# A state-exchange and feed-forward kernel: the first batch in a new order, one maximum for both halves, ScalarE's low words without a bias operand

## The chip, the cores and the metric

The kernel runs on one core of one Trainium2 chip. The metric is the device time of one execution in microseconds; lower is better. TensorE (PE) multiplies matrices, and its weight loads (PEld) run beside the products. VectorE (DVE) and ScalarE (ACT) do the elementwise work, GpSimd (POOL) almost nothing here, and SyncE (SP) issues nearly all transfers. A queue written SPq is SyncE's own sequence of transfers.

## The reference

The inputs are x (8 batches, 8 heads, 512 tokens, 64 features), state (8, 8, 32 rows, 64), moe_w_in (512 x 2048) and moe_w_out (2048 x 512), all float32. For each batch and head there are two attentions:

```
scores  = x state^T / 8;   a  = softmax(scores);   xread = a state      (512 tokens read 32 states)
scores2 = state x^T / 8;   a2 = softmax(scores2);  sread = a2 x         (32 states read 512 tokens)
```

The two results are joined to 544 rows a batch, with the heads side by side as 512 features, and go through a feed-forward layer: h = rows @ w_in; g = h where h >= 1, 0 where h <= -1, (h + 1)^2 / 4 between; out = g @ w_out. The output has 4352 rows of 512.

## The kernel before

**Tiling.** One batch's 512 tokens are the columns of its products. The hidden layer of 2048 is cut into 8 chunks j of 256. The product a @ (state @ w_in) is used in place of (a @ state) @ w_in: for each chunk, state @ w_in is made first (step sw, line 380). Values that must be exact are split into a high and a low part, and three products are added (lines 445 to 447 for the hidden layer, step p; lines 521 to 523 for the output, step g2). The state rows of all batches go through the layer as a ninth batch at the end.

**Steps of one chunk.** p.0.b.j and p.1.b.j are the two halves of the hidden product; relu (ACT, line 462), square (ACT, 466) and bound (DVE, 469) make u; gh (ACT, 478 and 620) and gl (DVE, 483) split it; g2.0 and g2.1 are the two halves of the output product. The two PSUM buffers of p come free when bound has read them. The weights come packed: the raw chunk i.c of w_in or o.c of w_out is loaded, its high words are scaled on ScalarE (high, line 575), its low words turned into small integers on ScalarE (line 567) or VectorE (562), and both are joined by VectorE (line 587: step w.c for w_in, join.c for w_out). woh.c and wol.c split the joined w_out. Raw chunks of w_in share two buffers, and a buffer comes free with step w of the chunk in it.

**Attention of one batch.** sc are the scores of both attentions at once (line 217). The first softmax goes turn (224), top1, less1, exp1, sum1, inv1, norm1, back (264), and ath and atl split its result. The second goes top2 (281 and 282: a maximum along the row, then a multiplication), exp2 (285), then a transpose of its result. In batch 0 TensorE transposes (e2p, kept.0). In every later batch VectorE transposes blocks of 32 x 32 (turn_blocks, line 310; steps blocks.1.0 and blocks.1.1 for batch 1), and then SyncE moves the blocks to their places with 16 transfers of 32 KB (shuffle, lines 312 to 324; step dma.eb.1). read2 (line 334) multiplies the result with the tokens xn, which SyncE loads (line 189; steps dma.xn.0 and dma.xn.1).

**Order.** All of batch 0, with the start of batch 1, is issued in an order written out by hand: SEQ holds one list of steps for each of SyncE, TensorE, VectorE and ScalarE, and each engine does its list strictly in that order. A planner (Plan.times, line 50) plays the lists with costs written beside each step and interleaves them; where TensorE would be idle between sc.0.1 and the first g2, it puts in filler matmuls (line 165), one for each 0.34 us planned. A step of the plan waits only for the steps named in its `after` list and for buffers. Nothing in the plan comes after dma.eb.1 or dma.xn.1. Their user is issued behind the plan, in the main loop: at chunk 0 of batch 1 the loop issues the hidden products of that chunk, then the places called "mid", and only then the output product of the chunk before (chunk 7 of batch 0). The line that puts read2 of batch 1 there is

```
    for name in ("read2", "scale2"):
        later("mid", 1, 0, (lambda name=name: getattr(atts[1], name)(),))
```

The shuffles and loads of later batches are issued by the main loop, which the change leaves alone.

Of the kernel before, what the change touches and what calls it, by code (L numbers as in the profile page):

```python
# [8 lines left out]
F32 = mybir.dt.float32  # L9
F32R = mybir.dt.float32r  # L10
I32 = mybir.dt.int32
U32 = mybir.dt.uint32
AF = mybir.ActivationFunctionType
ALU = mybir.AluOpType
# [5 lines left out]
NH = 1  # L20
NG = 0
SEQ = {
# [4 lines left out]
}  # L27
GROUPS = "0.1a 1.1a 2.1 3.2 5.2 7.2"

# [75 lines left out]
def state_exchange_moe(  # L105
# [49 lines left out]
    make_identity(nc, ident)  # L155
    half = small.tile([P, 1], F32, name="half")
    nc.vector.memset(half, 0.5)
    offset = small.tile([P, 1], F32, name="offset")
    nc.vector.memset(offset, 0.49)
    warmed = ps_acc("warmed")  # L160

    def warm(n):
# [29 lines left out]
    class Attention:  # L192
# [9 lines left out]
        def scores(self, half=None):  # L202
            b = self.b
            if half != 1:
                sc = ps_mm(f"sc{b}")
                self.sc = [sc[:, hh] for hh in range(2)]
                self.z = work.tile([P, 2, S], F32, tag="z", bufs=1, name=f"z{b}")
                self.m1 = small.tile([P, 2 * NM], F32, tag="m1", name=f"m1_{b}")
                self.s1 = small.tile([P, 2 * NM], F32, tag="s1", name=f"s1_{b}")
            for pr in range(NPR):  # L210
                for hh in range(2):
                    rows = slice(hh * 64, hh * 64 + 64)
                    o = self.sc[hh][pr * NS:(pr + 1) * NS]
                    m = self.xt[rows, :, pr]
                    if half is not None:
                        o, m = o[:, half * S // 2:(half + 1) * S // 2], m[:, half]
                    nc.tensor.matmul(o, lhsT=sb[rows, b, pr], rhs=m, start=True, stop=True)  # L217
# [56 lines left out]
        def top2(self, q):  # L274
            b = self.b
            if q == 0:
                self.e2 = work.tile([P, 2, S], F32, tag="e2", bufs=1, name=f"e2_{b}")
                self.nm2 = small.tile([P, 2], F32, tag="nm2", name=f"nm2_{b}")
                self.sum2 = small.tile([P, 2], F32, tag="sum2", name=f"sum2_{b}")
            nm = self.nm2[:, q:q + 1]  # L280
            nc.vector.tensor_reduce(out=nm, in_=self.sc[q], op=ALU.max, axis=AX.X, negate=True)
            nc.vector.tensor_scalar_mul(nm, nm, SCALE)

        def exp2(self, q):
            nc.scalar.activation(
# [272 lines left out]
    def low(kind, c, engine):  # L558

        lo = raws[kind, c][..., 0]  # L560
        if engine == "DVE":
            nc.vector.tensor_scalar(
                out=lo, in0=lo.bitcast(U32), scalar1=0.875 * 2.0 ** -29, scalar2=0.49,
                op0=ALU.mult, op1=ALU.add,
            )
        else:
            nc.scalar.activation(
                out=lo, in_=lo.bitcast(U32), func=AF.Relu, scale=0.875 * 2.0 ** -29, bias=offset
            )

    def high(kind, c):
# [114 lines left out]
    def att_ops2(b):  # L686
        def m(name, *a):
            return lambda *e: getattr(atts[b], name)(*a, *e)

        for q in range(2):  # L690
            k = (b, q)
            take = [("e2", ("e2", b))] if q == 0 else []
            op(("top2",) + k, "DVE", 0.75, m("top2", q), [("sc", b) if b else ("sc", b, 1)] + [("top2", b, 0)] * q, take=take)
            op(("exp2",) + k, "ACT", 0.66, m("exp2", q), [("top2",) + k], ends=[("sc", b)])
        if b:
            for q in range(2):
                op(("blocks", b, q), "DVE", 0.62, m("turn_blocks", q), [("exp2", b, q)] + [("blocks", b, 0)] * q,
                   take=[("tmp", ("eb", b))] if q == 0 else [])
            return
        op(("kept", b), "ACT", 0.95, m("keep_turned"), [("e2p", b)], ends=[("e2p", b)])  # L700
        op(("inv2", b), "DVE", 0.3, m("inv2"), [("exp2", b, 0), ("exp2", b, 1)])
        op(("rs", b), "DVE", 0.25, m("scale2"), [("sr", b), ("inv2", b)], ends=[("sr", b)])
        op(("srT", b), "ACT", 0.3, m("keep"), [("rt", b)], ends=[("rt", b)])
# [79 lines left out]

    tensor(("warm",), 4.5, lambda: warm(WARM))
    for side in range(2):
        tensor(("sc", 0, side), 0.6, lambda side=side: att_start(0, side), [("dma", "xt", 0, side)],
               take=[("mm", ("sc", 0))] * (1 - side), ends=[("xt", 0)])
    att_ops1(0)
    att_ops2(0)
# [158 lines left out]
```

## Time and profile before

| | |
|---|---|
| median of three runs | 647.79 us (647.2 to 647.85) |
| the profiled execution | 647.15 us |
| its span | 645.4 us |
| TensorE busy | 635.2 us, 98% of the span |
| VectorE, ScalarE busy | 354.5 us, 370.6 us |
| TensorE's granted clock | 1.00 |
| HBM read, written | 34.08 MB, 8.91 MB |

The span runs from the first to the last record of the profile; the execution's own time is 1.75 us longer. In a timeline row the columns are start and duration in us, engine, line, operation, output and inputs, their shapes, how many instructions are merged, and in brackets the idle time before them with what ended it. In a group's row the figures behind the bar are the busy time in us and the mean of one instruction in ns, and behind the next bar the engine's idle time before them. In a row of waits they are the total in us, how often, and the longest. In a row of transfers the last figure is the median time in us from issue to landing.

### The profile page before, as it was taken

What the parts mean: (1) busy time and instruction counts of PE and PEld (TensorE: products, weight loads), DVE (VectorE), ACT (ScalarE), POOL (GpSimd) and SP (SyncE); (2) the same over time, 40 slices, a digit from 0 to 9 for tenths busy, and PEclk for the clock granted to TensorE, in tenths of its full rate; (3) what the DMA queues carried; (4) which work ended last, traced back from release to release, by engine and by line L of the source; (5) the groups of instructions that cost most, each with busy time, mean ns of one, the idle gap of its engine ahead of it and who ended that gap; (6) DMA issues with size and microseconds to landing.
All of it is one profiled execution on the core that took longest, in us unless ns stands there. A gap on an engine that the chain in (4) does not pass through costs nothing.

```text
span 645.4 us, 10351 instructions
## 1 busy us (share of the span) xinstructions
PE 635.2 (98%) x4358; PEld 509.6 (79%) x4358; DVE 354.5 (55%) x508; ACT 370.6 (57%) x535; POOL 0.8 (0%) x7
## 2 busy tenths in 40 slices
PE   7999999999999999999999999999999999999997
PEld 5577777878787878878787878878787878788896
DVE  6999955664356535673366534663456543335431
ACT  5999755555655555545655465545755464544641
POOL 0000000000000000000000000000000000000000
PEclk9999999999999999999999999999999999999999
DMA  8996114011211102011302102011102000000101
GB/s 356 414 371 259 19 26 187 7 28 66 87 46 32 68 28 103 11 24 66 126 6 34 66 34 98 17 36 49 66 0 34 1 37 30 2 0 1 66 1 33
DMA packets 41550, 47.33 MB, mean 73 GB/s; under 512 B 31776, under 2 KB 31904, under 8 KB 38432
## 3 DMA queue, kind: packets, MB, share of 16 engines
q1 hardware_dynamic: 41168, 46.35, 20.8%
q8 instruction: 34, 0.56, 0.4%
q10 hardware_dynamic: 336, 0.33, 0.2%
q14 instruction: 12, 0.10, 0.1%
HBM read 34.08 MB, written 8.91 MB: 67 GB/s over the span
## 4 chain that ended last, share of the span: by engine, by line
PE 93%; ACT 3%; DVE 2%; DMA 1%; issue 0%; SPq 0%
PE acc L521 19%; PE acc L522 19%; PE acc L523 19%; PE h L445 10%; PE h L446 10%; PE h L447 10%; PE sw L380 4%; PE sc L217 1%; PE sr L334 1%; DMA sb<-in_state_dram 1%; ACT u L462 1%; ACT raw_i L575 0%; DVE w L587 0%; ACT raw_o L575 0%; ACT gh L620 0%
## 5 line engine op out<-in xcount | busy, mean ns | idle before, releaser
L521 PE MATMUL acc<-wo,gh 128*128 128x512 f32 x544 | 214.3, 394 | 0.0
L522 PE MATMUL acc<-wo,gh 128*128 128x512 f32 x544 | 212.1, 390 | 0.1
L523 PE MATMUL acc<-wo,gl 128*128 128x512 f32 x544 | 211.8, 389 | 0.0
L469 DVE SCALAR_TENSOR_TENSOR u<-u,h 128x512 f32<-128x512 f32 x136 | 92.7, 686 | 193.6 <-ACT u L466 193.6
L462 ACT ACTIVATE u<-h,half 128x512 f32<-128x512 f32 x136 | 93.1, 689 | 168.3 <-PE h L447 166.0
L521 PEld LDWEIGHTS acc<-wo,gh 128*128 128x128 f32 x544 | 102.1, 188 | 29.1 <-issue 6.6
L483 DVE TENSOR_TENSOR gl<-u,gh 128x1024 fp32r<-128x1024 f32 x68 | 83.3, 1225 | 75.7 <-ACT gh L620 75.6
L523 PEld LDWEIGHTS acc<-wo,gl 128*128 128x128 f32 x544 | 102.1, 188 | 21.6
L522 PEld LDWEIGHTS acc<-wo,gh 128*128 128x128 f32 x544 | 102.2, 188 | 20.8 <-DVE wo L605 0.4
L620 ACT CAST gh<-u 128x1024 fp32r<-128x1024 f32 x68 | 71.4, 1049 | 40.7 <-DVE u L469 40.7
L466 ACT ACTIVATE u<-u 128x512 f32<-128x512 f32 (+1 forms) x128 | 84.4, 660 | 3.9
L380 PE MATMUL sw<-w,sb 64*32 64x256 f32 x1024 | 33.5, 380 | 1.5 <-DVE w L587 1.5
L380 PEld LDWEIGHTS sw<-w,sb 64*32 64x32 f32 x1024 | 17.9, 106 | 16.1 <-issue 9.7
L536 ACT COPY o<-acc 128x512 f32<-128x512 f32 x33 | 19.0, 586 | 20.0 <-PE acc L523 20.0
L445 PE MATMUL h<-ath,sw_5h 128*128 128x512 f32 x64 | 25.6, 400 | 0.0
L446 PE MATMUL h<-ath,sw_3l 128*128 128x512 f32 x64 | 25.0, 391 | 0.2 <-DVE sw_3l L407 0.2
L445 PE MATMUL h<-ath,sw_3h 128*128 128x512 f32 x64 | 25.0, 391 | 0.0
L446 PE MATMUL h<-ath,sw_5l 128*128 128x512 f32 x64 | 25.0, 390 | 0.0
L447 PE MATMUL h<-atl,sw_3h 128*128 128x512 f32 x64 | 24.9, 390 | 0.0
L447 PE MATMUL h<-atl,sw_5h 128*128 128x512 f32 x64 | 24.9, 389 | 0.0
L445 PE MATMUL h<-ath,sw_1h 128*128 128x512 f32 x60 | 23.5, 391 | 0.6 <-DVE u L469 0.6
L445 PE MATMUL h<-ath,sw_7h 128*128 128x512 f32 x60 | 23.9, 399 | 0.0
(158 smaller groups left out, 700.1 us busy)
## 6 DMA issues: line engine op xcount, KB each, us to landing
xt<-in_xt_dram SPq DMA_DIRECT2D x16, 512.0 KB, 4.7
raw_i<-in_moe_w_in_dram SPq DMA_DIRECT2D x8, 1024.0 KB, 7.7
raw_o<-in_moe_w_out_dram SPq DMA_DIRECT2D x8, 1024.0 KB, 9.8
xn<-in_x_dram SPq DMA_DIRECT2D x8, 1024.0 KB, 5.0
out_dram<-o SPq DMA_DIRECT2D x32, 256.0 KB, 2.0
e<-eb SPq DMA_DIRECT2D x112, 32.0 KB, 2.0
sb<-in_state_dram SPq DMA_DIRECT2D x1, 448.0 KB, 11.4
out_dram<-o SPq DMA_DIRECT2D x4, 64.0 KB, 1.8
```

The costliest lines, as they stand in the source:

```text
L380: nc.tensor.matmul(banks[hh][pr * NS:(pr + 1) * NS, i * CI:(i + 1) * CI], lhsT=sb[rows, bi, pr], rhs=w32[ci][rows, pr], start=True, stop=True,
L445: nc.tensor.matmul(o, lhsT=wh[:, k, sl], rhs=ah[:, k], start=first, stop=False)
L446: nc.tensor.matmul(o, lhsT=wl[:, k, sl], rhs=ah[:, k], start=False, stop=False)
L447: nc.tensor.matmul(o, lhsT=wh[:, k, sl], rhs=al[:, k], start=False, stop=last)
L462: nc.scalar.activation(out=self.u[:, i], in_=self.hs[i], func=AF.Relu, scale=0.5, bias=half)
L466: nc.scalar.activation(out=u, in_=u, func=AF.Square)
L469: nc.vector.scalar_tensor_tensor(out=self.u[:, i], in0=self.u[:, i], scalar=1.0, in1=self.hs[i], op0=ALU.min, op1=ALU.max,)
L483: nc.vector.tensor_tensor(out=gl, in0=self.u, in1=gh.bitcast(F32), op=ALU.subtract)
L521: nc.tensor.matmul(a, lhsT=lh, rhs=oh, start=f == 0, stop=False)
L522: nc.tensor.matmul(a, lhsT=lh, rhs=ol, start=False, stop=False)
L523: nc.tensor.matmul(a, lhsT=ll, rhs=oh, start=False, stop=f == NF - 1)
L620: nc.scalar.copy(out=out, in_=src)
```

## The change

SEQ gets new lists for all four engines. Among much else:

- SyncE fetches i.2 before i.1, and xn.1 moves from between o.4 and i.6 to the last place, behind dma.eb.1.
- TensorE does e2p.0 directly after sw.0.0, sr.0 ahead of p.0.0.1, and both halves of each g2 together.
- VectorE does blocks.1.1 between bound.0.0.7 and back.1.1, at the end of its list. It stood between gl.0.5 and wol.7.
- ScalarE takes low.i.0, low.i.2, low.i.7, low.o.4, low.o.5, ath.0.0 and woh.5 from VectorE and gives up low.o.0, low.o.2, low.o.3, swh.0.5 and woh.7 to it. In all it turns 11 of the 16 low words instead of 9.

In batches 0 and 1 the maximum of the second softmax is taken for both halves by one instruction (top2_both), and both exponentials wait for it. Batches 2 to 7 keep the form with one instruction for each half. ScalarE's low words get another scale and no bias, and the constant for the bias is dropped. The plan now says that sc.0.1 waits for the two turns of the first half.

```diff
--- before.py
+++ after.py
@@ -20,10 +20,10 @@
 NH = 1
 NG = 0
 SEQ = {
-    "SP": "dma.xt.0.0 dma.xt.0.1 dma.i.0 dma.i.1 dma.o.0 dma.sb.1 dma.xn.0 dma.i.2 dma.o.1 dma.xt.1 dma.i.3 dma.o.2 dma.i.4 dma.o.3 dma.i.5 dma.o.4 dma.xn.1 dma.i.6 dma.o.5 dma.i.7 dma.o.6 dma.o.7 dma.xt.2 dma.eb.1",
-    "PE": "warm sc.0.0 sc.0.1 sw.0.0 p.0.0.0 p.1.0.0 sw.0.1 e2p.0 p.0.0.1 p.1.0.1 sw.0.2 g2.0.0.0 sr.0 p.0.0.2 p.1.0.2 g2.1.0.0 sw.0.3 g2.0.0.1 p.0.0.3 p.1.0.3 sc.1 g2.1.0.2 g2.0.0.2 rt.0 p.0.0.4 p.1.0.4 g2.1.0.1 sw.0.5 g2.1.0.3 g2.0.0.3 p.0.0.5 p.1.0.5 sw.0.7 g2.0.0.4 p.0.0.6 p.1.0.6 g2.1.0.4 g2.1.0.5 p.0.0.7 p.1.0.7 g2.0.0.5 g2.0.0.6 g2.1.0.6",
-    "DVE": "turn.0.0.0 turn.0.1.0 top1.0.0.0 top1.0.1.0 turn.0.0.1 turn.0.1.1 top1.0.0.1 top1.0.1.1 less1.0.0 less1.0.1 low.i.0 sum1.0.0 sum1.0.1 w.0 inv1.0 top2.0.0 norm1.0.0 norm1.0.1 back.0.0 w.1 back.0.1 top2.0.1 ath.0.0 atl.0.1 atl.0.0 join.0 low.i.2 swl.0.1 inv2.0 bound.0.0.0 bound.1.0.0 w.2 gl.0.0 wol.0 swl.0.2 low.i.3 w.3 bound.0.0.1 bound.1.0.1 rs.0 join.1 low.i.4 gl.0.1 w.4 wol.1 join.2 bound.0.0.2 bound.1.0.2 swl.0.3 wol.2 gl.0.2 low.o.4 join.3 woh.3 top2.1.0 turn.1.0 top2.1.1 bound.0.0.3 bound.1.0.3 turn.1.1 w.5 wol.3 gl.0.3 w.6 join.4 top1.1.1 low.o.5 bound.0.0.4 bound.1.0.4 low.i.7 wol.4 swl.0.5 gl.0.4 w.7 less1.1.1 join.5 blocks.1.0 woh.5 sum1.1.1 wol.5 bound.0.0.5 bound.1.0.5 swl.0.7 join.7 gl.0.5 blocks.1.1 wol.7 join.6 bound.1.0.6 bound.0.0.6 top1.1.0 wol.6 gl.0.6 less1.1.0 sum1.1.0 inv1.1 norm1.1.0 norm1.1.1 back.1.0 bound.0.0.7 back.1.1 bound.1.0.7 atl.1.0 atl.1.1 gl.0.7",
-    "ACT": "high.i.0 exp1.0.0 exp1.0.1 high.i.1 low.i.1 swh.0.0 exp2.0.0 high.o.0 low.o.0 ath.0.1 exp2.0.1 relu.0.0.0 relu.1.0.0 swh.0.1 square.0.0 high.i.2 kept.0 gh.0.0 woh.0 high.o.1 swh.0.2 relu.0.0.1 relu.1.0.1 high.i.3 square.0.1 low.o.1 low.o.2 gh.0.1 high.i.4 woh.1 relu.0.0.2 relu.1.0.2 high.o.2 square.0.2 swh.0.3 woh.2 gh.0.2 high.o.3 low.o.3 low.i.5 relu.0.0.3 relu.1.0.3 high.i.5 square.0.3 exp2.1.0 exp2.1.1 high.i.6 high.o.4 gh.0.3 low.i.6 srT.0 high.o.5 relu.0.0.4 relu.1.0.4 square.0.4 woh.4 high.i.7 swh.0.5 gh.0.4 high.o.6 low.o.6 high.o.7 low.o.7 relu.0.0.5 exp1.1.1 relu.1.0.5 square.0.5 swh.0.7 gh.0.5 woh.7 relu.0.0.6 relu.1.0.6 square.0.6 woh.6 gh.0.6 relu.0.0.7 exp1.1.0 relu.1.0.7 square.0.7 ath.1.0 ath.1.1 gh.0.7",
+    "SP": "dma.xt.0.0 dma.xt.0.1 dma.i.0 dma.i.2 dma.o.0 dma.i.1 dma.o.1 dma.xn.0 dma.i.4 dma.sb.1 dma.i.3 dma.o.3 dma.o.2 dma.xt.1 dma.o.4 dma.o.7 dma.i.6 dma.i.5 dma.i.7 dma.o.6 dma.xt.2 dma.o.5 dma.eb.1 dma.xn.1",
+    "PE": "warm sc.0.0 sc.0.1 sw.0.0 e2p.0 p.0.0.0 p.1.0.0 sw.0.2 sw.0.1 sr.0 p.0.0.1 p.1.0.1 g2.0.0.0 g2.1.0.0 sw.0.3 p.0.0.2 p.1.0.2 g2.0.0.1 g2.1.0.1 p.0.0.3 sc.1 p.1.0.3 g2.0.0.2 g2.1.0.2 rt.0 p.0.0.4 p.1.0.4 sw.0.5 g2.0.0.3 g2.1.0.3 p.0.0.5 p.1.0.5 sw.0.7 g2.1.0.4 p.0.0.6 p.1.0.6 g2.0.0.4 g2.1.0.5 p.0.0.7 p.1.0.7 g2.0.0.5 g2.0.0.6 g2.1.0.6",
+    "DVE": "turn.0.1.0 turn.0.0.0 top1.0.1.0 top1.0.0.0 turn.0.1.1 turn.0.0.1 top2.0 top1.0.1.1 top1.0.0.1 less1.0.1 less1.0.0 w.0 sum1.0.0 sum1.0.1 inv1.0 norm1.0.0 back.0.0 norm1.0.1 low.o.0 back.0.1 atl.0.0 w.2 w.1 join.0 atl.0.1 swl.0.2 swl.0.1 bound.1.0.0 bound.0.0.0 wol.0 gl.0.0 low.i.3 low.i.4 w.4 w.3 inv2.0 join.1 rs.0 bound.0.0.1 bound.1.0.1 wol.1 low.o.2 gl.0.1 join.2 low.o.3 swl.0.3 wol.2 bound.1.0.2 bound.0.0.2 join.4 gl.0.2 join.3 top2.1 w.5 woh.3 turn.1.1 turn.1.0 bound.0.0.3 wol.3 bound.1.0.3 top1.1.0 w.6 gl.0.3 blocks.1.0 top1.1.1 less1.1.0 less1.1.1 swh.0.5 swl.0.5 bound.1.0.4 bound.0.0.4 wol.4 w.7 gl.0.4 sum1.1.1 join.5 bound.1.0.5 bound.0.0.5 swl.0.7 wol.5 gl.0.5 sum1.1.0 inv1.1 join.6 bound.0.0.6 bound.1.0.6 wol.6 gl.0.6 join.7 norm1.1.1 woh.7 wol.7 norm1.1.0 back.1.0 bound.1.0.7 bound.0.0.7 blocks.1.1 back.1.1 gl.0.7 atl.1.1 atl.1.0",
+    "ACT": "high.i.0 low.i.0 exp2.0.0 exp2.0.1 exp1.0.1 exp1.0.0 high.i.2 low.i.2 high.o.0 swh.0.0 ath.0.0 low.i.1 high.i.1 kept.0 ath.0.1 relu.0.0.0 relu.1.0.0 swh.0.2 swh.0.1 square.0.0 woh.0 gh.0.0 high.i.4 low.o.1 high.i.3 high.o.1 relu.0.0.1 relu.1.0.1 square.0.1 woh.1 high.o.2 gh.0.1 swh.0.3 relu.0.0.2 relu.1.0.2 square.0.2 woh.2 high.o.4 low.o.4 high.o.3 gh.0.2 low.i.6 low.i.5 high.i.6 high.i.5 relu.1.0.3 relu.0.0.3 exp2.1.0 square.0.3 exp2.1.1 low.o.7 gh.0.3 srT.0 high.i.7 relu.1.0.4 relu.0.0.4 square.0.4 high.o.6 low.i.7 woh.4 low.o.5 low.o.6 gh.0.4 exp1.1.1 high.o.5 relu.1.0.5 relu.0.0.5 square.0.5 swh.0.7 exp1.1.0 woh.5 gh.0.5 relu.1.0.6 relu.0.0.6 square.0.6 woh.6 gh.0.6 high.o.7 relu.0.0.7 relu.1.0.7 square.0.7 gh.0.7 ath.1.0 ath.1.1",
 }
 GROUPS = "0.1a 1.1a 2.1 3.2 5.2 7.2"
 
@@ -155,8 +155,6 @@
     make_identity(nc, ident)
     half = small.tile([P, 1], F32, name="half")
     nc.vector.memset(half, 0.5)
-    offset = small.tile([P, 1], F32, name="offset")
-    nc.vector.memset(offset, 0.49)
     warmed = ps_acc("warmed")
 
     def warm(n):
@@ -202,7 +200,7 @@
         def scores(self, half=None):
             b = self.b
             if half != 1:
-                sc = ps_mm(f"sc{b}")
+                sc = self.both = ps_mm(f"sc{b}")
                 self.sc = [sc[:, hh] for hh in range(2)]
                 self.z = work.tile([P, 2, S], F32, tag="z", bufs=1, name=f"z{b}")
                 self.m1 = small.tile([P, 2 * NM], F32, tag="m1", name=f"m1_{b}")
@@ -280,6 +278,14 @@
             nm = self.nm2[:, q:q + 1]
             nc.vector.tensor_reduce(out=nm, in_=self.sc[q], op=ALU.max, axis=AX.X, negate=True)
             nc.vector.tensor_scalar_mul(nm, nm, SCALE)
+
+        def top2_both(self):
+            b = self.b
+            self.e2 = work.tile([P, 2, S], F32, tag="e2", bufs=1, name=f"e2_{b}")
+            self.nm2 = small.tile([P, 2], F32, tag="nm2", name=f"nm2_{b}")
+            self.sum2 = small.tile([P, 2], F32, tag="sum2", name=f"sum2_{b}")
+            nc.vector.tensor_reduce(out=self.nm2, in_=self.both, op=ALU.max, axis=AX.X, negate=True)
+            nc.vector.tensor_scalar_mul(self.nm2, self.nm2, SCALE)
 
         def exp2(self, q):
             nc.scalar.activation(
@@ -565,7 +571,7 @@
             )
         else:
             nc.scalar.activation(
-                out=lo, in_=lo.bitcast(U32), func=AF.Relu, scale=0.875 * 2.0 ** -29, bias=offset
+                out=lo, in_=lo.bitcast(U32), func=AF.Relu, scale=0.9375 * (2.0 ** -29 - 2.0 ** -49)
             )
 
     def high(kind, c):
@@ -687,11 +693,9 @@
         def m(name, *a):
             return lambda *e: getattr(atts[b], name)(*a, *e)
 
+        op(("top2", b), "DVE", 1.3, m("top2_both"), [("sc", b) if b else ("sc", b, 1)], take=[("e2", ("e2", b))])
         for q in range(2):
-            k = (b, q)
-            take = [("e2", ("e2", b))] if q == 0 else []
-            op(("top2",) + k, "DVE", 0.75, m("top2", q), [("sc", b) if b else ("sc", b, 1)] + [("top2", b, 0)] * q, take=take)
-            op(("exp2",) + k, "ACT", 0.66, m("exp2", q), [("top2",) + k], ends=[("sc", b)])
+            op(("exp2", b, q), "ACT", 0.66, m("exp2", q), [("top2", b)], ends=[("sc", b)])
         if b:
             for q in range(2):
                 op(("blocks", b, q), "DVE", 0.62, m("turn_blocks", q), [("exp2", b, q)] + [("blocks", b, 0)] * q,
@@ -783,7 +787,8 @@
 
     tensor(("warm",), 4.5, lambda: warm(WARM))
     for side in range(2):
-        tensor(("sc", 0, side), 0.6, lambda side=side: att_start(0, side), [("dma", "xt", 0, side)],
+        tensor(("sc", 0, side), 0.6, lambda side=side: att_start(0, side),
+               [("dma", "xt", 0, side)] + [("turn", 0, q, 0) for q in range(2)] * side,
                take=[("mm", ("sc", 0))] * (1 - side), ends=[("xt", 0)])
     att_ops1(0)
     att_ops2(0)
```

## The prediction

> **What bounds the kernel now.** I read the page first (busy time, the chain that ended last, DMA issues), then what TensorE waited for, then busy time by windows, then the timeline of batch 0.
>
> ```profile
> PE 635.2 (98%) x4358; PEld 509.6 (79%) x4358; DVE 354.5 (55%) x508; ACT 370.6 (57%) x535; POOL 0.8 (0%) x7
> PE 93%; ACT 3%; DVE 2%; DMA 1%; issue 0%; SPq 0%
> ```
> ```profile
> PE sw L380 <- DVE w L587: 1.5, 1, 1.5
> PE warmed L165 <- POOL ident masks.py:199: 1.4, 1, 1.4
> PE h L445 <- DVE u L469: 1.0, 2, 0.6
> PE sc L217 <- DVE z L224: 0.9, 1, 0.9
> PE h L457 <- DVE zt L264: 0.9, 1, 0.9
> PE h L446 <- DVE sw_3l L407: 0.2, 1, 0.2
> ```
> ```profile
> 0.00:20.00 20.00, 15.15 (x118) 10.53 (x118) 13.71 (x30) 11.56 (x17) 0.83 (x7) 1.00 0.91 364
> 20.00:40.00 20.00, 18.92 (x203) 13.91 (x203) 18.19 (x25) 19.99 (x25) 0.00 (x0) 1.00 1.01 419
> 40.00:60.00 20.00, 19.84 (x125) 14.49 (x124) 19.65 (x27) 19.77 (x26) 0.00 (x0) 1.00 0.67 260
> 60.00:80.00 20.00, 20.00 (x117) 15.93 (x116) 19.97 (x25) 16.28 (x18) 0.00 (x0) 1.00 0.30 100
> 80.00:100.00 20.00, 20.00 (x216) 15.29 (x215) 12.47 (x20) 11.77 (x18) 0.00 (x0) 1.00 0.17 43
> ```
>
> TensorE makes up 93% of the chain, and the list of its waits is complete: six kinds, 5.9 us together. The windows (columns: window, its length, busy time of PE, PEld, DVE, ACT, POOL, granted clock, DMA share, GB/s) put them all before 60 us. From there on PE is full in every window. So two things count: how early batch 0 gets PE going, and whether PE ever waits again. A wait added after 60 us adds to the end in full, because nothing later has slack to give back.
>
> **The change part by part.** *Low words without the bias.* The nearest row of ScalarE with the same strided shape and no pointer operand is the high words' one.
>
> ```profile
> L575 ACT ACTIVATE raw_o<-raw_o 128x1024 f32<-128x1024 f32 x8 | 9.3, 1158 | 0.0
> L567 ACT ACTIVATE raw_o<-raw_o,offset 128x1024 int32<-128x1024 uint32 x6 | 7.3, 1240 | 0.0
> L281 DVE TENSOR_REDUCE nm<-sc 128x1 f32<-128x512 f32 x4 | 2.6, 654 | 0.0
> L282 DVE TENSOR_SCALAR nm<-nm 128x1 f32<-128x1 f32 x4 | 0.6, 154 | 0.1
> L483 DVE TENSOR_TENSOR gl<-u,gh 128x1024 fp32r<-128x1024 f32 x8 | 9.8, 1224 | 0.1
> ```
>
> 1240 becomes about 1158 ns, 0.08 us each. The new list gives ScalarE 11 such words instead of 9, so ScalarE does 11 x 1.16 = 12.8 us where it did 9 x 1.24 = 11.2; VectorE gives up two. *One maximum for both halves.* Two reductions and two multiplications cost 2 x (0.65 + 0.15) = 1.6 us; one of 1024 elements lies near the 1.22 us of the 1024-element row, plus 0.15: 1.4 us. That is 0.2 us a batch, in batches 0 and 1 only (the others keep the single form), and the first half's exponential now waits for both. Neither edit reaches PE by itself: both lie inside the work of DVE and ACT, which hides them. If it did not, they are worth some tenths either way.
>
> *The order up to 80 us.* I walked the new lists with the pitches of the rows.
>
> ```profile
> 19.46 1.35 ACT L462 ACTIVATE u<-h,half 128x512 f32<-128x512 f32 x2
> 16.40 3.68 PE L457 MATMUL h<-zt,sw_0w 128*128 128x512 f32 x8 [0.93 <-DVE zt L264]
> 23.60 0.50 PE L445 MATMUL h<-ath,sw_1h 128*128 128x512 f32 x1 [0.56 <-DVE u L469]
> 30.48 1.10 PE L334 MATMUL sr<-xn,e 128*32 128x64 f32 x64
> 32.00 0.50 PE L445 MATMUL h<-ath,sw_2h 128*128 128x512 f32 x1 [0.42 <-DVE u L469]
> ```
>
> The second input chunk fetched is now i.2, and i.1 takes a raw buffer that w.0 frees near 12.7 us, so I let it land about 5 us after that, near 17.6 (in the old list it stood ahead of every wait). On ScalarE its two words stand ahead of kept.0 and of the first relu, which then starts near 21 us rather than 19.5; p.0.0.1 follows near 26 instead of 23.60. Against that, sr.0 and sw.0.1 are done before it, and g2.1.0.0 comes straight behind g2.0.0.0: by my walk near 31.7 us, where the old order had done the same products at 30.48 + 1.10 = 31.6 and began its next one at 32.00. So the start is a wash. Later DVE and ACT are as full as before, and I find PE short of operands by some tenths at p.0.0.4, sw.0.5, p.0.0.5 and p.0.0.6. Net I take +0.5 us at the end of batch 0, with bounds of -1.1 (the two stalls on the bounds of u, 0.56 + 0.42, and the last 0.2 all gone) and +3 (one raw buffer handed over late to i.7, whose high word stands ahead of the relu of chunk 4 on ScalarE). Filler matmuls change in number, but stand where PE waits anyway.
>
> *What SyncE and VectorE do last in batch 0.* Here lies the large term. Three steps are moved that no PE step of the list waits for, but read2 of batch 1 does (line 334; it is issued in the main loop behind the first products of batch 1): the second block transpose blocks.1.1, the 16 shuffle transfers dma.eb.1 that wait for both transposes, and the load dma.xn.1.
>
> ```profile
> 32.27 0.38 SPq L189 DMA_DIRECT2D xn<-in_x_dram  x1
> 74.31 10.54 SPq L322 DMA_DIRECT2D e<-eb  x16
> ```
> ```profile
> 73.57 0.71 DVE L310 STREAM_TRANSPOSE eb<-e 128x512 f32<-128x512 f32 x1
> 76.70 1.28 DVE L469 SCALAR_TENSOR_TENSOR u<-u,h 128x512 f32<-128x512 f32 x2
> 82.05 0.68 ACT L462 ACTIVATE u<-h,half 128x512 f32<-128x512 f32 x1
> 82.76 1.06 ACT L466 ACTIVATE u<-u 128x1024 f32<-128x1024 f32 x1
> 81.03 0.39 PE L447 MATMUL h<-atl,sw_7h 128*128 128x512 f32 x1
> 81.26 0.39 PE L521 MATMUL acc<-wo,gh 128*128 128x512 f32 x1
> 92.23 1.10 PE L334 MATMUL sr<-xn,e 128*32 128x64 f32 x64
> ```
> ```profile
> SPq L322 <- DVE eb L310: 16.0, 1, 16.0
> ```
> ```profile
> xn<-in_x_dram SPq DMA_DIRECT2D x8, 1024.0 KB, 5.0
> e<-eb SPq DMA_DIRECT2D x112, 32.0 KB, 2.0
> ```
>
> Before, xn.1 was issued at 32.27 and the shuffle at 74.31, right behind the transpose that it waited for (16.0 us), and was all issued by 84.85; landed 2.0 us later, it was 5 us ahead of read2 at 92.23. In the new lists blocks.1.1 stands behind bound.0.0.7, and SyncE issues dma.eb.1 and only then dma.xn.1. Call T the moment when PE passes p.1.0.7 (81.26 before). From T the new order needs: 0.2 until relu.1.0.7 starts (the last matmul ends at 81.42), 0.7 to the square, 1.06 for it, 1.28 for the two bounds, 0.71 for blocks.1.1: T + 3.95. Then 16 issues, 10.54: T + 14.5. Then xn.1, 5.0 to land: T + 19.5. PE has the same work between T and read2 in both orders (three halves of g2 and the two products of batch 1), 92.23 - 81.26 = 10.97 us. So PE waits 19.5 - 10.97 = 8.5 us. Behind the waiting matmul on PE stand the g2 of chunk 7 and the whole rest; nothing of it overtakes. T cancels: whatever the walk of batch 0 is worth, this wait comes on top. Its lower bound, were xn.1 to land like the small transfers (2.0), is 5.5; its upper bound, were DVE still busy when the square ends (norm1.1.0 and back.1.0 stand in front of the bounds), about 9.8.
>
> *TensorE after such a wait.* PE has no idle time over 1.5 us in any row of before, so the restart is bounded by the start of the kernel.
>
> ```profile
> 1.45 3.36 PE L165 MATMUL warmed<-ident 128*128 128x128 f32 x14 [1.45 <-POOL ident masks.py:199]
> 4.86 1.11 PE L217 MATMUL sc<-xt,sb 64*32 64x256 f32 x16
> 6.91 0.67 PE L217 MATMUL sc<-xt,sb 64*32 64x256 f32 x16 [0.94 <-DVE z L224]
> 7.51 4.29 PE L165 MATMUL warmed<-ident 128*128 128x128 f32 x36
> 13.27 0.67 PE L380 MATMUL sw<-w,sb 64*32 64x256 f32 x16 [1.48 <-DVE w L587]
> ```
>
> The same small matmul took 3.36/14 = 0.240 us at first and 4.29/36 = 0.119 later, the same 16 score matmuls 1.11 and then 0.67: a cold start costs 14 x 0.121 + 0.44 = 2.1 us. After 1.48 us idle 16 matmuls took 0.67 again, so a short pause costs nothing. Bounds for 8.5 us idle: 0 and 2.1; I take 2.1, since the pause is far longer than the one shown to be free. (The granted clock reads 1.00 in the first window too; the halving is seen in the durations alone.) The Trainium skill speaks against the change here: "TensorE: Matmul & The Clock Gate", Part 1 ("What's actually happening"), says that the array falls to half clock after at least one idle window of about 3.4 us and returns after about 3.4 us of work. By that rule the restart would cost an estimated 1.7 us or somewhat more, and the total would be 0.4 less than mine; no run here shows an idle time that long.
>
> *Sum.* +0.5 + 8.5 + 2.1 = +11.1 us. The profiled execution took 647.15 us (span 645.4 and 1.75 around it), so it would become 658.25; the median of the three runs is 0.64 above it, hence 658.9.
>
> **The rivals.** *No cold restart.* PE resumes at full speed: +9.0, 656.8. For it: the 1.48 us pause was free. Against it: the pause would be almost six times as long. *A second wait in batch 0.* i.7's raw buffer is the one that w.6 frees, not w.5, so ScalarE stands at high.i.7 and p.0.0.5 starts late: about 2.5 more, 661.4. For it: DVE and ACT are at 98% and 99% of their time from 40 to 60. Against: the plan itself counts buffers, whichever comes free. *Not slower: the late read is hidden.* The transfers leave in another order than the list's, or read2 is reached later than I think; only the walk is left. Decisive is whether xn.1 and the last shuffle land within 10.97 us of T, which needs them 8.5 us sooner. Then at its best the two stalls at 23.6 and 32.0 go: 647.8 - 1.1 = 646.7, no measurable difference. Against it: before, SyncE's transfers left in exactly the order of its list.
>
> **How the numbers follow.** The forecast (wait and cold restart) gets 0.70, no cold restart 0.14, the second wait 0.10, hidden 0.04, another cause of slowing 0.02. The range reaches from 655.5 (wait at 8.5 without a restart, walk at -0.8) to 661.5 (the second wait). A measurement of this kernel can tell about 0.2%, 1.3 us, from no change. Slower: 0.95; within it: 0.03; faster, if the walk gains more than its bound: 0.02.
>
> **What would show it right or wrong.** In the profile after: a new PE wait of 8 to 9 us at L334, released by the transfer xn, some 11 us behind the last product of chunk 7; the shuffle issued behind the last bound, xn.1 behind it; the next matmuls of 512 columns about twice as long for some 3 us; ScalarE's low words near 1.16 us; one reduction near 1.2 us. No wait at L334 would make the forecast wrong at its core; a wait released by the shuffle would show xn.1 sized wrongly.

## The result, and the profile after

The changed kernel takes 663.4 us (median of six runs, 662.82 to 668.22), the kernel before 647.27 us (six runs, 647.11 to 647.85). The ratio is 1.0258, with a 95% interval of 1.0246 to 1.0271: slower by 16 us. The profiled execution took 663.0 us, its span is 661.2 us, 15.8 us more than before. The sign and the place were forecast; the size was not, and the result lies above the range.

From the page after: the span, the busy times, TensorE's granted clock in 40 slices, and the chain by engine.

```profile
span 661.2 us, 10357 instructions
PE 639.6 (97%) x4364; PEld 513.2 (78%) x4364; DVE 354.7 (54%) x501; ACT 371.0 (56%) x537; POOL 0.8 (0%) x7
...
PEclk9999996999999999999999999999999999999999
...
PE 83%; DVE 5%; ACT 4%; DMA 4%; SPq 1%; issue 1%; ACTq 0%; DVEq 0%
```

TensorE's share of the chain fell from 93% to 83%; transfers, VectorE and ScalarE took the rest. One slice, the seventh (99 to 116 us), shows a lower clock.

All that TensorE waited for after (line, releaser; us in total, how often, longest):

```profile
PE sr L340 <- DMA xn<-in_x_dram: 10.3, 1, 10.3
PE sw L386 <- DVE rs L348: 2.3, 1, 2.3
PE warmed L163 <- POOL ident masks.py:199: 1.4, 1, 1.4
PE sc L215 <- DVE z L222: 0.9, 1, 0.9
PE sr L340 <- DVE sw_1l L413: 0.7, 1, 0.7
PE h L451 <- DVE u L475: 0.6, 1, 0.6
PE rt L354 <- ACT e L291: 0.5, 1, 0.5
PE h L453 <- DVE atl L268: 0.4, 1, 0.4
PE sw L386 <- DVE w L593: 0.2, 1, 0.2
```

The first row is the forecast wait (read2 is line 340 in the new file). Two moments cut the 15.8 us into three. T is when TensorE passes p.1.0.7, that is, the start of the first output product behind it. read2 of batch 1 starts later.

| | before | after | difference | forecast |
|---|---|---|---|---|
| T | 81.26 | 84.39 | +3.1 | +0.5 |
| T to the start of read2 | 10.97 | 21.99 | +11.0 | +8.5 |
| start of read2 to the end of the span | 553.17 | 554.82 | +1.65 | +2.1 |

**T to read2.** From the timelines of TensorE, ScalarE, VectorE and SyncE after (start, duration):

```profile
84.39 0.39 PE L527 MATMUL acc<-wo,gh 128*128 128x512 f32 x1
93.54 0.50 PE L453 MATMUL h<-atl,sw_7h 128*128 128x512 f32 x1 [0.37 <-DVE atl L268]
106.38 2.26 PE L340 MATMUL sr<-xn,e 128*32 128x64 f32 x64 [10.29 <-DMA xn<-in_x_dram]
```
```profile
85.32 1.06 ACT L472 ACTIVATE u<-u 128x1024 f32<-128x1024 f32 x1
```
```profile
83.48 1.22 DVE L593 SCALAR_TENSOR_TENSOR wf<-raw_o 128x1024 int32<-128x1024 int32 x1
84.61 0.68 DVE L255 TENSOR_TENSOR z<-z,s 128x512 f32<-128x512 f32 x1
85.22 0.69 DVE L624 CAST wo<-wf 128x1024 fp32r<-128x1024 f32 x1
85.94 1.23 DVE L611 TENSOR_TENSOR wo<-wf,wo 128x1024 fp32r<-128x1024 f32 x1
87.08 0.68 DVE L255 TENSOR_TENSOR z<-z,s 128x512 f32<-128x512 f32 x1
87.80 0.71 DVE L262 STREAM_TRANSPOSE zt<-z 128x512 f32<-128x512 f32 x1
88.43 1.25 DVE L475 SCALAR_TENSOR_TENSOR u<-u,h 128x512 f32<-128x512 f32 x2
89.60 0.69 DVE L316 STREAM_TRANSPOSE eb<-e 128x512 f32<-128x512 f32 x1
```
```profile
90.36 10.50 SPq L328 DMA_DIRECT2D e<-eb  x16
100.91 0.60 SPq L187 DMA_DIRECT2D xn<-in_x_dram  x1
```

The square is done at 85.32 + 1.06 = 86.38, which is T + 1.99, as forecast. But the bounds do not start then. VectorE works without a break through join.7, norm1, woh.7, wol.7, norm1.1.0 and back.1.0, and takes up the bounds at 88.43, 2.05 us late. Then all runs in series: bounds and the block transpose 1.93 us, the 16 issues 10.55, and from the issue of xn.1 to the start of read2 5.47. The sum is 1.99 + 2.05 + 1.93 + 10.55 + 5.47 = 21.99 us.

**T itself.** VectorE, TensorE and SyncE in the timeline, around 31 us:

```profile
30.91 1.30 DVE L568 TENSOR_SCALAR raw_i<-raw_i 128x1024 int32<-128x1024 uint32 x2 [2.39 <-DMA raw_i<-in_moe_w_in_dram]
32.31 2.36 DVE L593 SCALAR_TENSOR_TENSOR w<-raw_i 128x1024 int32<-128x1024 int32 x2
...
36.01 0.28 DVE L348 TENSOR_TENSOR rs<-sr,r 128x128 f32<-128x128 f32 x1
```
```profile
36.35 1.10 PE L386 MATMUL sw<-w,sb 64*32 64x256 f32 x32 [2.27 <-DVE rs L348]
```
```profile
21.56 0.33 SPq L561 DMA_DIRECT2D raw_i<-in_moe_w_in_dram  x1
```

Chunk i.3 is issued at 21.56 and lands only at 30.9. VectorE waits 2.39 us for it, then does both low words, w.4, w.3, inv2.0 and join.1, and only behind these rs.0, which reads the PSUM tile of sr.0. sw.0.3 needs that buffer, and TensorE stands 2.27 us. The idle time is not the whole account: a filler matmul counts as busy and hides a wait too. The rows of the fillers by line, of before and of after (busy us, mean ns):

```profile
L165 PE MATMUL warmed<-ident 128*128 128x128 f32 x74 | 10.8, 308 | 1.4 <-POOL ident masks.py:199 1.4
```
```profile
L163 PE MATMUL warmed<-ident 128*128 128x128 f32 x80 | 13.1, 328 | 1.4 <-POOL ident masks.py:199 1.4
```

Before T, idle time and fillers together are 5.9 + 10.8 = 16.7 us before and 6.6 + 13.1 = 19.7 us after (6.6 is the list of waits without the rows of xn and atl, which come behind T). The difference, 3.0, accounts for the 3.1 by which T came later. Up to 27 us, with the last filler done in both, the two kernels stand some 0.2 apart (16.3 after: waits of 1.4 + 0.9 + 0.7 + 0.2 and the fillers; 16.1 before: the waits but for 0.4 at 32.00 and the 0.2, and the fillers); the rest is lost behind that, 2.3 of it at sw.0.3.

**The restart.** Windows after, with the granted clock in the third figure from the end:

```profile
99.00:100.00 1.00, 0.00 (x0) 0.00 (x0) 0.00 (x0) 0.00 (x0) 0.00 (x0) 0.72 0.35 56
106.30:108.00 1.70, 1.62 (x54) 1.65 (x58) 0.00 (x0) 0.00 (x0) 0.00 (x0) 0.50 0.00 0
109.00:110.00 1.00, 1.00 (x4) 0.76 (x4) 0.00 (x0) 0.00 (x0) 0.00 (x0) 0.66 0.00 0
110.00:111.00 1.00, 1.00 (x6) 0.81 (x5) 0.00 (x0) 0.24 (x1) 0.00 (x0) 1.00 0.00 0
```

TensorE is idle from 96.1. The clock falls to a half in the window from 99 to 100 (a mean of 0.72 puts it near 99.4, 3.3 us after the last product) and is back in the one from 109 to 110 (0.66, near 109.7, 3.3 us after the restart). The 64 small products of read2 took 2.26 us where they had taken 1.10.

**The two instruction edits.** From the groups by line of the first 100 us after:

```profile
L573 ACT ACTIVATE raw_i<-raw_i 128x1024 int32<-128x1024 uint32 x6 | 6.9, 1165 | 0.9 <-DMA raw_i<-in_moe_w_in_dram 0.9
L573 ACT ACTIVATE raw_o<-raw_o 128x1024 int32<-128x1024 uint32 x5 | 5.6, 1134 | 0.0
```
```profile
L287 DVE TENSOR_REDUCE nm<-sc 128x2 f32<-128x1024 f32 x2 | 2.4, 1199 | 0.0
```

A low word takes 1134 to 1165 ns where it took 1240 (w_out's) or 1284 (w_in's), and one maximum 1199 ns where two took 2 x 654.

### The profile page after: what moved, and what is told of

It reads as the page before. It is cut to its first block, busy times and chain, and to the rows that moved or that the text cites. A ratio compares the mean times of both kernels' runs of the same rounds, so it can differ in the third digit from the quotient of the medians.

```text
span 661.2 us, 10357 instructions
## 1 busy us (share of the span) xinstructions
PE 639.6 (97%) x4364; PEld 513.2 (78%) x4364; DVE 354.7 (54%) x501; ACT 371.0 (56%) x537; POOL 0.8 (0%) x7
## 4 chain that ended last, share of the span: by engine, by line
PE 83%; DVE 5%; ACT 4%; DMA 4%; SPq 1%; issue 1%; ACTq 0%; DVEq 0%
PE acc L527 17%; PE acc L528 17%; PE acc L529 17%; PE h L451 9%; PE h L452 9%; PE h L453 9%; PE sw L386 4%; DMA raw_i<-in_moe_w_in_dram 2%; SPq L328 1%; PE sr L340 1%; PE sc L215 1%; DVE w L593 1%; DVE u L475 1%; DMA xn<-in_x_dram 1%; ACT u L468 1%
## 5 line engine op out<-in xcount | busy, mean ns | idle before, releaser
L453 PE MATMUL h<-atl,sw_7h 128*128 128x512 f32 x60 | 23.5, 392 | 0.4 <-DVE atl L268 0.4
```

The lines of the kernel that those rows point to most:

```text
L453: nc.tensor.matmul(o, lhsT=wh[:, k, sl], rhs=al[:, k], start=False, stop=last)
```

## The experiments

The theory: read2's inputs come late because blocks.1.1 and xn.1 stand last in their lists. The rivals: the rest of the new order loses the time (PSUM buffers, the late i.3), the instruction edits do, or the restart does. All kernels start from one of the two shown; lists are cut to where they change, and "before" in each comparison is the kernel before on the same chip.

**xn_ahead**: after, the load of the tokens ahead of the shuffle.

```diff
 SP
- dma.o.5 dma.eb.1 dma.xn.1
+ dma.o.5 dma.xn.1 dma.eb.1
```

> The changed kernel with one step moved: SyncE loads the tokens of batch 1 (dma.xn.1) ahead of the 16 shuffle transfers (dma.eb.1) and not behind them. Theory (the inputs of read2 of batch 1 come late): the wait at the sr product is then ended by the last shuffle, issued near 100.3 us and landed 2.0 us later, near 102.3 where the tokens landed at 106.3; the wait of 10.3 us falls to about 6.3 and the time to about 659.4 us. First rival (the shuffle alone is late and the load costs nothing, since it would land meanwhile): no change, 663. Second rival (the new order of batch 0 costs most of the 16 us, and PE would be short somewhere else): less than 1.5 us gained.

Measured: 658.98 (one run). Its waits of TensorE at read2:

```profile
PE sr L340 <- DMA e<-eb: 4.9, 4, 4.2
PE sr L340 <- DMA xn<-in_x_dram: 1.5, 1, 1.5
```

The releaser changes to the shuffle and 4.4 us go. Not all goes: the 16 issues still start behind the last block transpose.

**blocks_early**: after, blocks.1.1 some 12 us earlier on VectorE; xn.1 stays last.

```diff
 DVE
- gl.0.5 sum1.1.0 ... bound.0.0.7 blocks.1.1 back.1.1
+ gl.0.5 blocks.1.1 sum1.1.0 ... bound.0.0.7 back.1.1
```

> The changed kernel with one step moved: VectorE does the second block transpose of batch 1 (blocks.1.1) right behind gl of chunk 5 of batch 0, and not behind the last bound of chunk 7; the tokens are still loaded behind the shuffle. Theory: transpose near 78 us, shuffle issued by about 88.7, tokens landed near 94, ahead of read2 at 96. The whole wait of 10.3 us goes, and with it the cold restart of about 1.75: 663.4 - 12.0 = 651.4 us, give or take 0.8; what is left over the kernel before is what the new order of batch 0 costs, 3 to 4 us. Rival (the new order costs most of it): above 657. Rival (the restart costs nothing): 653.

Measured: 650.81 (649.87 to 651.72, four runs), against before 1.0049 [1.0032, 1.0066]. SyncE and TensorE in its timeline:

```profile
78.49 11.07 SPq L328 DMA_DIRECT2D e<-eb  x16
```
```profile
96.73 1.10 PE L340 MATMUL sr<-xn,e 128*32 128x64 f32 x64
```

One moved step of 0.7 us is worth 12.6 us: neither the shuffle nor xn.1 is waited for, the 64 products run at full clock (1.10), and from there to the end it is 649.9 - 96.73 = 553.17 us, as before. What is left, 3.75 us over before by the medians, is the rest of the change. xn.1 still stands last here and costs nothing there: its place counts only once the shuffle is late.

**before_tail**: before, with the tail of the new lists alone.

```diff
 DVE
- gl.0.5 blocks.1.1 wol.7 ... bound.1.0.7 atl.1.0
+ gl.0.5 wol.7 ... bound.1.0.7 blocks.1.1 atl.1.0
 SP
- dma.o.4 dma.xn.1 dma.i.6 ... dma.xt.2 dma.eb.1
+ dma.o.4 dma.i.6 ... dma.xt.2 dma.eb.1 dma.xn.1
```

> The kernel before with only the end of its lists as in the change: blocks.1.1 behind the last bound of chunk 7, and the tokens of batch 1 loaded last on SyncE, behind the shuffle. Both edits of instructions and all the rest of the new order are left out. Theory: the last bound of chunk 7 ends near 87.2 us here, the shuffle is issued from 87.9 to 98.4, the tokens land near 103.7, PE stands at the sr product from 92.2: 11.5 us of wait and 1.75 of restart, 647.3 + 13.2 = 660.5 us. Rival (the new order of batch 0 costs most of the 16 us): under 652.

Measured: 661.11 (660.3 to 661.57, four runs), 1.0211 [1.0196, 1.0227]. In its timeline:

```profile
87.63 10.52 SPq L322 DMA_DIRECT2D e<-eb  x16
```
```profile
103.53 2.26 PE L334 MATMUL sr<-xn,e 128*32 128x64 f32 x64 [10.90 <-DMA xn<-in_x_dram]
```

The tail alone costs 14.0 us in an order that is otherwise the old one. Taken out of the new kernel (12.6, by the one step blocks.1.1) and put into the old one (14.0, by blocks.1.1 and xn.1), it gives nearly the same: the cause is shown from both sides.

**before_edits**: before's order with both instruction edits (the maximum for both halves stands where that of the first half stood).

```diff
- func=AF.Relu, scale=0.875 * 2.0 ** -29, bias=offset
+ func=AF.Relu, scale=0.9375 * (2.0 ** -29 - 2.0 ** -49)
 DVE
- inv1.0 top2.0.0 norm1.0.0 ... back.0.1 top2.0.1 ath.0.0
+ inv1.0 top2.0 norm1.0.0 ... back.0.1 ath.0.0
- top2.1.0 turn.1.0 top2.1.1 bound.0.0.3
+ top2.1 turn.1.0 bound.0.0.3
```

> The kernel before, its order kept, with only the two edits of instructions: ScalarE's low words without the bias operand, and one maximum for both halves in batches 0 and 1 (it stands where the first half's maximum stood). Theory (both lie inside work that TensorE does not wait for): within 0.5 us of the kernel before. Rival (the edits themselves cost part of the 3.7 us that are left when the late transpose is mended, since the first half's exponential now waits for the whole maximum): 1 us or more slower.

Measured: 647.25 (11 runs) against 647.28 (20 runs), 0.9999 [0.9991, 1.0008]. In the old order the edits are worth nothing, within some 0.6 us either way. That they cost nothing in the new order too, and that the planner's new rule for sc.0.1 does not count, was not tested; with that reserve the 16 us is order.

**kept_busy**: after, with 42 float32 products of the identity (84 matmuls in the profile) into columns of sr that nobody reads, ahead of read2 of batch 1. Nothing is left out.

```diff
             sr = self.sr = ps_mm(f"sr{b}")
+            for _ in range(42 * (b == 1)):
+                nc.tensor.matmul(sr[:, 0, P:2 * P], lhsT=ident, rhs=ident, start=True, stop=True)
```

> The changed kernel with 42 filler products of the identity on TensorE, 128 columns each, directly ahead of the sr product of batch 1, written to columns that nothing reads. They take about 42 x 2 x 0.119 = 10 us, just the wait. Theory (the sr product and three more run cold after the wait): the wait for the tokens shrinks to under 0.5 us, their landing stays, the sr product takes 1.1 us again instead of 2.26, and the time falls by about 1.7 us to 661.7. Rival (the slow start behind the wait has another cause, or costs nothing): 663 to 664.

Measured: 662.86 (one run); by the time alone the rival (663 to 664) is nearer than the theory (661.7). In its timeline:

```profile
107.58 1.41 PE L342 MATMUL sr<-xn,e 128*32 128x64 f32 x64 [1.08 <-DMA xn<-in_x_dram]
```

The granted clock is 1.00 from 94 to 116 us, the small products take 1.41 us, not 2.26, and from the start of read2 to the end it is 661.1 - 107.58 = 553.52 us, 1.3 less than after. The total shows little of it, since T came 1.0 us later in this execution (85.42). Its own trace says why. Behind the wait at sw.0.3, which was 2.34 us here and 2.27 in after, the clock fell (window, and a product inside it):

```profile
38.00:39.00 1.00, 1.00 (x4) 0.81 (x3) 1.00 (x2) 1.00 (x2) 0.00 (x0) 0.50 0.99 418
39.56 0.63 PE L455 MATMUL h<-atl,sw_2h 128*128 128x512 f32 x1
```

It is 0.50 from about 37.7 to 41.1 us, though the work had gone on at 36.42. The twelve products of p.0.0.2 and p.1.0.2 took 4.45 us (37.45 to 41.90) where after, at a clock of 1.00, took 2.85 (37.38 to 40.23): 1.6 us lost, of which 0.5 comes back at rt.0, where TensorE does not wait in this execution. So the restart is real and makes 1.3 of the 1.65 us in the third row of the table above, and a pause of 2.3 us can bring on such a loss too, in one execution and not in another.

**bounds_first**: after, with the two steps of the first softmax moved from ahead of the last bounds.

```diff
 DVE
- wol.7 norm1.1.0 back.1.0 bound.1.0.7 bound.0.0.7 blocks.1.1 back.1.1
+ wol.7 bound.1.0.7 bound.0.0.7 blocks.1.1 norm1.1.0 back.1.0 back.1.1
```

> The changed kernel with two steps moved on VectorE: norm1.1.0 and back.1.0 stand behind blocks.1.1 and not ahead of the two bounds of chunk 7. Theory (in the changed kernel the bounds began at 88.43 us, though the square was done at 86.38, because these two steps, themselves behind the joining of the last output chunk, held VectorE; the chain bounds, transpose, 16 issues, load is serial from there): the bounds begin near 87.2, right behind wol.7, and all of the chain comes 1.3 us earlier; the wait for the tokens falls from 10.3 to 9.0, the split of the first softmax is done no later than before, and the time falls from 663.4 to about 662.1 us. Rival (the wait is set by something that does not hang on VectorE, the issue of earlier transfers or the load's own landing): 663 to 664.

Measured: 662.08 (661.25 to 663.28, four runs), 1.0222 [1.0204, 1.0241]. VectorE and TensorE:

```profile
86.95 1.28 DVE L475 SCALAR_TENSOR_TENSOR u<-u,h 128x512 f32<-128x512 f32 x2
```
```profile
105.06 2.26 PE L340 MATMUL sr<-xn,e 128*32 128x64 f32 x64 [9.23 <-DMA xn<-in_x_dram]
```

The bounds start 1.48 us sooner and read2 1.32 us sooner. Of both, 0.13 us is an earlier T (84.26). The square ends at 86.24, so VectorE is 0.71 us late where it was 2.05: the busy VectorE was part of the wait. The median is 1.3 us lower, and the intervals of the two ratios do not meet. The profiled execution, 661.0, shows less of it: from read2 to the end it is 555.94 us there, 1.1 more than after, since the half clock lasted longer (last section).

**The rest of the order.** Five further kernels start from blocks_early.

rs_early frees the PSUM buffer of sr.0 sooner:

```diff
 DVE
- gl.0.0 low.i.3 low.i.4 w.4 w.3 inv2.0 join.1 rs.0 bound.0.0.1
+ gl.0.0 inv2.0 rs.0 low.i.3 low.i.4 w.4 w.3 join.1 bound.0.0.1
```

> The mended kernel (blocks.1.1 behind gl of chunk 5) with two more steps moved on VectorE: inv2.0 and rs.0, which empties the PSUM buffer of the sr product of batch 0, stand directly behind gl of chunk 0, where VectorE was idle, and not behind join.1. Theory (TensorE stood 1.9 to 2.3 us at sw.0.3 because the sr product held the one buffer until rs.0, and rs.0 stood behind words that waited for the chunk i.3): sw.0.3 then waits only for w.3, some 1.6 us earlier, and the time falls from 650.8 to about 649.2 us. Rival (w.3 and w.4 come as late, or VectorE and ScalarE are behind anyway): no change.

sb_only moves the state of the later batches ahead of i.1, so that i.3 is issued sooner:

```diff
 SP
- dma.o.0 dma.i.1 dma.o.1 dma.xn.0 dma.i.4 dma.sb.1 dma.i.3
+ dma.o.0 dma.sb.1 dma.i.1 dma.o.1 dma.xn.0 dma.i.4 dma.i.3
```

> The mended kernel with one transfer moved on SyncE: the 448 KB of states for the later batches (dma.sb.1) go ahead of i.1, into the time from 13.4 to 15.5 us in which the DMA engines have nothing queued, and not between i.4 and i.3. Theory (the new order of fetches leaves the DMA engines idle once at the start and so lands i.3 late, at 30.9, with both vector engines waiting for it): i.3 lands about 1.1 us earlier, and the time falls to about 649.7 us. Rival (the late i.3 does not set the pace): no change.

rs_sb has both:

> The mended kernel with both of these moves. Theory: they add up, since w.3 follows i.3 and sw.0.3 then waits for w.3 alone: about 648.1 us. Rival: no more than the better one of the two.

mended_two is sb_only with rs.0 between w.3 and join.1, and with the split of batch 1's first softmax ahead of gh.0.7 and gl.0.7:

```diff
 DVE
- w.3 inv2.0 join.1 rs.0 bound.0.0.1 ... back.1.1 gl.0.7 atl.1.1 atl.1.0
+ w.3 inv2.0 rs.0 join.1 bound.0.0.1 ... back.1.1 atl.1.1 atl.1.0 gl.0.7
 ACT
- gh.0.7 ath.1.0 ath.1.1
+ ath.1.0 ath.1.1 gh.0.7
```

> The kernel with the transpose mended and the states loaded ahead of i.1, and two more places mended: inv2.0 and rs.0 stand between w.3 and join.1 on VectorE, and at the end of batch 0 the split of the first softmax of batch 1 (ath.1, atl.1) stands ahead of gh and gl of chunk 7 on both vector engines, as in the kernel before. Theory (what is left over the kernel before are single TensorE waits, each ended by one step that stands too late in the new lists): the waits of 0.5 us at sw.0.3 and 0.6 us at the first product of batch 1 go, 649.7 - 1.1 = 648.6 us. Rival (ScalarE and VectorE are simply behind in the new order, and a wait that is removed comes back at the next step): no gain over 649.7.

mended_all is mended_two with batch 1's turns ahead of w.5, and join.5 and high.o.5 behind the bounds and the square of chunk 5:

```diff
 DVE
- top2.1 w.5 woh.3 turn.1.1 turn.1.0 bound.0.0.3 ... join.5 bound.1.0.5 bound.0.0.5 swl.0.7
+ top2.1 turn.1.1 turn.1.0 w.5 woh.3 bound.0.0.3 ... bound.1.0.5 bound.0.0.5 join.5 swl.0.7
 ACT
- exp1.1.1 high.o.5 relu.1.0.5 relu.0.0.5 square.0.5 swh.0.7
+ exp1.1.1 relu.1.0.5 relu.0.0.5 square.0.5 high.o.5 swh.0.7
```

> The same with two more places mended: the turns of batch 1 stand ahead of w.5, where VectorE waited 0.45 us, and join.5 and high.o.5 stand behind the bounds and the square of chunk 5. Theory: the waits of 0.5 us at rt.0 and 0.6 us at p.0.0.6 go too, 647.5 us, level with the kernel before. Rival: no gain over the one with two places mended, or a loss, because the steps put back are then late themselves.

Measured, with the account of each profiled execution (idle and fillers before T; issue and landing time of i.1):

| | median us (runs) | ratio to before | T | idle + fillers | T to read2 | i.1 |
|---|---|---|---|---|---|---|
| blocks_early | 650.81 (4) | 1.0049 [1.0032, 1.0066] | 84.83 | 7.3 + 12.9 | 11.90 | 13.11, 4.6 |
| rs_early | 651.25 (4) | 1.0054 [1.0040, 1.0068] | 84.46 | 8.3 + 11.8 | 11.88 | 12.40, 7.2 |
| sb_only | 649.66 (5) | 1.0041 [1.0028, 1.0053] | 82.48 | 4.6 + 13.3 | 11.87 | 13.10, 4.7 |
| rs_sb | 649.79 (8) | 1.0041 [1.0031, 1.0052] | 82.80 | 6.4 + 11.8 | 11.92 | 12.78, 5.0 |
| mended_two | 649.61 (5) | 1.0034 [1.0021, 1.0046] | 83.51 | 7.1 + 11.8 | 10.98 | 12.79, 6.4 |
| mended_all | 650.37 (5) | 1.0046 [1.0033, 1.0060] | 84.49 | 7.8 + 11.7 | 11.37 | 12.24, 6.0 |

sb_only's time came out as expected (649.7). VectorE's row for i.3 and TensorE's at sw.0.3:

```profile
28.97 1.30 DVE L568 TENSOR_SCALAR raw_i<-raw_i 128x1024 int32<-128x1024 uint32 x2 [0.61 <-DMA raw_i<-in_moe_w_in_dram]
```
```profile
34.41 1.10 PE L386 MATMUL sw<-w,sb 64*32 64x256 f32 x32 [0.48 <-DVE rs L348]
```

i.3 lands 2.4 us sooner than in blocks_early (31.38) and 1.9 sooner than in after, and the wait at sw.0.3 falls from 1.9 (in blocks_early) to 0.5. rs_early missed (649.2 expected). The wait for rs.0 is gone, but others stand in its list of waits:

```profile
PE sw L386 <- DVE w L593: 1.5, 1, 1.5
PE sw L386 <- ACT e L305: 1.4, 1, 1.4
```

The first of them, ahead of sw.0.0, is no new loss: blocks_early has 0.4 there, and 1.1 us more of fillers in front of it. The second is kept.0, which stands on ScalarE behind both words of i.1; i.1 landed late in that execution. rs_sb, mended_two and mended_all missed as well (648.1, 648.6 and 647.5 expected). mended_two did what it was built for at the end (T to read2 is 10.98, as in before), and yet gained nothing in the median; in mended_all waits for the bounds come back. Their row (sb_only has one of 0.6):

```profile
PE h L451 <- DVE u L475: 1.5, 3, 0.6
```

So the late i.3 is a likely part of the rest, and not a settled one. The same move of sb.1 was made twice and gained both times, 1.15 us from blocks_early to sb_only and 1.46 from rs_early to rs_sb, but the intervals of the ratios overlap in both pairs. Single runs scatter by as much: in rs_sb two of the eight, 651.20 and 651.26, have a mean clock of 0.996 where the others have 0.999 or 1.0. Of what is left then, some 2.4 us, the account says only that it sits in waits and fillers of the start, which move from one engine to another as each is removed. No single step was shown to cause them, and no version tried was faster than the kernel before.

## Why the prediction was wrong in size

**The direction and the mechanism held.** The wait at read2, released by xn; the shuffle behind the last bound and xn.1 behind it; the restart at half speed: each is in the profile, and blocks_early and before_tail show that the tail alone makes 12.6 to 14.0 of the 16 us. That T cancels held too: in before_tail T is 81.59 and read2 starts 21.94 us later, in after 84.39 and 21.99. That the two agree so closely is in part chance, since other steps hold VectorE there (back.1.0 and back.1.1; the shuffle is issued at T + 6.04 and T + 5.97).

**"So PE waits 19.5 - 10.97 = 8.5 us": mis-sized, measured 11.0.** The step that failed is T + 3.95 for the block transpose; it was done at T + 5.9 (89.60 + 0.69 - 84.39). The prediction took the bounds as starting when the square ends and set VectorE's own list down as an upper bound only, of 9.8. VectorE was busy, for 2.05 us and not for the 1.3 of the two steps then named, because join.7, woh.7 and wol.7 stood in front as well. bounds_first took away 1.34 of it (2.05 to 0.71) by moving two steps. The second part is the transfer: 5.47 us from issue to use, not 5.0. The issue of the 16 was right (10.55 against 10.54).

**"Net I take +0.5 us at the end of batch 0": wrong, measured +3.1, and at the upper bound.** The start was indeed a wash (0.2 up to 27 us; p.0.0.1 at 25.64 against 26 forecast, i.1 landed at 18.0 against 17.6). What failed came after: i.3 landed at 30.9, which the walk did not cost, and rs.0 stands behind join.1, so that a PSUM buffer came late and TensorE stood 2.27 us. That much the trace shows; what each of the two is worth in the end stays open, since rs_early took that wait away and gained nothing, and the gain of sb_only is not clear of the scatter. The upper bound of +3 was given to another mechanism, the raw buffer of i.7; its wait at p.0.0.5 does not exist, as the complete list of waits shows, and that its figure was nearly met is luck.

**"I take 2.1" for the restart: measured 1.65.** In the execution that the table shows, the estimate of 1.7 from the Trainium skill ("TensorE: Matmul & The Clock Gate", Part 1) was nearer than the bound from the start of the kernel. The trace agrees with its rule in the size of the step (0.50). In before_tail the half clock lasted 5.5 us after the restart (103.53 to 109.0), and the part from read2 to the end was 2.6 us longer than in before (659.3 - 103.53 against 553.17). The same page says that the window runs freely, so that such counts differ between runs; the executions agree with that. They do not agree with its idle time of about 3.4 us: the clock fell 2.7 us after the last product in before_tail, and in kept_busy after a pause of only 2.34 us. So the prediction's "a short pause costs nothing", read from one pause of 1.48 us, holds for that pause and cannot be carried to one of 2.3.

**The rivals.** "No cold restart" falls with the clock of 0.50, "hidden" with the wait itself, and the second wait with the list of waits.

**Low words and maximum: right.** 1134 to 1165 ns against 1158, 1199 against 1220, and nothing at the end of the kernel, shown by before_edits.

Why the range missed: its upper end took the second wait alone, on top of a wait at 8.5. The wait at its own bound of 9.8, with the walk at +3 and 2.1 for the restart, would have made 662.7, still 0.7 below the measured time, since the wait came out 1.2 us over its bound. The three terms were bounded each by itself, but all three could come out high together, and two of them did.

## What to carry to other kernels

A list that is balanced for the stage it covers can be wrong at its edge: look for every user outside the list, ask which steps feed it, and cost the last steps of each queue in series, for here 0.7 us of work placed last held back 16 issues of 0.66 us and a load behind them. Cost a step at the end of an in-order list from the moment its engine gets there, not from the moment its input is ready. When TensorE's lists of waits are compared, add the filler matmuls to the idle time: only the sum explains where the end moved.

## What the runs showed of the hardware beyond that

- A pause of TensorE can cost more than its length, and not always the same: the granted clock fell to 0.50 some 2.7 us (before_tail), 3.0 us (xn_ahead), 3.3 us (after) or 4.7 us (bounds_first) after the last product, and stayed there for 3.3 us (after) to 5.7 us (bounds_first, 105.06 to 110.8) once the work went on. What the restart cost is about half of that time: 1.65 us of 3.3 (after), 2.6 of 5.5 (before_tail), 2.8 of 5.7 (bounds_first). In kept_busy a pause of 2.34 us was enough: the clock fell 1.3 us after the work had gone on, stayed at 0.50 for 3.4 us and cost 1.6 us, while in after a pause of 2.27 us cost nothing of the kind. One of the six runs of the changed kernel, at 668.22, has a mean clock of 0.984 where the others have 0.989 to 0.991; it was not profiled.
- A load that was issued earlier need not land earlier. i.1, issued at 13.1 to 13.4 us in five executions of the new order, landed 4.6 to 4.8 us after; issued at 12.2 to 12.8 us in five others, it took 4.6, 5.0, 6.0, 6.4 and 7.2 us. The 4.6 (bounds_first, issued at 12.34) and the 7.2 (rs_early, at 12.40) come from the same SyncE list. Why was not tested.
- Sixteen small transfers from one queue are bound by their issue: 10.5 us for 16 of 32 KB, 0.66 us each, while each lands 1.9 us after its own issue.
